# A padded 33rd head: zeros by GpSimd in place of 20 matmul columns per product

## The chip, the cores and the metric

The kernel runs on one core of a Trainium2 chip. The metric is the device time of one execution in microseconds; the median of three runs is given. A profiled execution shows what each engine did: TensorE (PE, with its weight loads as PEld), VectorE (DVE), ScalarE (ACT), GpSimd (POOL) and SyncE (SP, which issues the DMAs).

## The reference

One block of 2048 tokens with 640 features goes through a linear attention (A) and a gated feed-forward network (B), and a sigmoid gate for each token mixes the two. All inputs are bf16.

```python
qkv = (x @ wqkv).reshape(B, S, 3, H, Dh)                # H = 32 heads of Dh = 20
pq = einsum("bhsd,hdf->bhsf", q, w_phi)
pk = einsum("bhsd,hdf->bhsf", k, w_phi)
phi_q = concatenate([softmax(pq), softmax(-pq)], -1)    # 40 features a head
phi_k = concatenate([softmax(pk), softmax(-pk)], -1)
kv = einsum("bhsf,bhsd->bhfd", phi_k, v)
num = einsum("bhqf,bhfd->bhqd", phi_q, kv)
den = einsum("bhqf,bhf->bhq", phi_q, phi_k.sum(s)) + 1e-6
a = (num / den).reshape(B, S, D) @ wo
b = (silu(x @ w_gate) * (x @ w_up)) @ w_down            # F = 1728
g = sigmoid((x * gate_w).sum(-1))
out = g * a + (1 - g) * b
```

## The kernel before

**Tiles and stages.** Tokens are worked in 16 tiles of 128, in 4 blocks of 512. x lies transposed in `xT` (640 features as 5 chunks of 128 partitions). A short `premult` stage multiplies the k and q weights by `w_phi`, so that `wqk` turns x directly into the features' logits. For each block come 4 v tiles, 4 k tiles and the k-v product, summed in `kvacc`; from some 120 us on come 16 q tiles. The feed-forward network (`ffn`: gate and up for 14 column blocks, `down`) runs over the same 4 blocks in between, as the low-priority work of TensorE.

**A k or q tile** (`features`, L799). TensorE multiplies the token tile by `wqk[:, which]`: 5 matmuls of 512 columns into one PSUM bank and 5 short ones into the next. The bank pair is read as 33 heads of 20 logits (`HP = 33`, `pv` and `pg`, 660 columns), in 11 groups of 3 heads (`NG = 11`, `GH = 3`), since a group's 3 x 40 = 120 features fit 128 partitions once transposed. There are only 32 heads. For the 33rd place the first of the short matmuls is 148 columns wide: `over` (L795) runs 20 columns on into the next chunk's weights, so that the place holds finite numbers. VectorE takes maximum and minimum of each head (L831, L835), subtracts them into the slot `phi` (L839, L843), ScalarE takes the exponential, VectorE the sums (L854) and reciprocals (L858), and GpSimd normalizes in place (`f_nm`, L864). Later the rows of the 33rd place are multiplied away by the mask `kvm`, or meet no column.

**What follows.** For k: `kvpart` multiplies 4 tiles' `phi` with `v1` in two halves, groups 0 to 5 and 6 to 10. For q: SP transposes the slot by DMA into `eT`, TensorE multiplies by `kvsb` (`num`), VectorE divides (L946 to L955), SP transposes `ob` into `oT`, TensorE multiplies by `wo`, and the result is mixed and stored.

**Order.** Nothing is placed by hand: every piece of work is a task with a cost in us, dependencies, a priority and buffers to take and give back (`_Plan`, L229). The planner goes through time, and each engine that is free takes the first task of its list that can start. Feature products also have an earliest time (`hold`, L812), and transposes get some slack on top of their cost. The order found this way is written into the instruction streams; at run time an engine waits only for semaphores. The tracker (`_Tracker.run`, L160) derives these waits from the addresses read and written, within one engine too. All TensorE work is issued by one helper (`mms`, L420), so its line is L434 everywhere; memsets are issued at L454, ScalarE's at L444, DMAs at L462. `pair` is a pair of PSUM banks, `st` one of 3 sets of maxima, sums and so on, `phi` one of 11 slots, `us` one of 3 buffers for the up half of the feed-forward network. The `st` set is given back when the task `norm` ends.

Of the kernel before, what the change touches and what calls it, by code (L numbers as in the profile page):

```python
# [6 lines left out]
P = 128  # L7
S_TOK = 2048
D = 640
H = 32  # L10
DH = 20
# [6 lines left out]
NG = 11  # L18
GF = GH * 2 * DH
# [16 lines left out]
class _Tracker:  # L36
# [123 lines left out]
    def run(self, eng, fn, reads=(), writes=(), semname=None, inc=None):  # L160
        rkeys = [self._key_of(a) for a in reads]
        wkeys = [self._key_of(a) for a in writes]
        need = {}

        def req(ev):
            if ev is None:
                return
            s, v = ev
            if v > need.get(s, 0):
                need[s] = v  # L170

        for k in rkeys:
            for kk in self._conflicts(k):
                req(self.lastw[kk])
        for k in wkeys:
            for kk in self._conflicts(k):
                req(self.lastw[kk])
                for s, v in self.readers[kk].items():
                    req((s, v))
        self._emit_waits(eng, need)  # L180
        ins = fn()
        if semname is None:
            semname = {"pe": "pe", "act": "act", "dve": "dve", "pool": "pool"}[eng]
            if inc is None:
                inc = 1
        elif semname == "dma":
            semname = self.new_dma_sem()
            inc = 16
        ins.then_inc(self.sem[semname], inc)
        self.cnt[semname] += inc  # L190
        v = self.cnt[semname]
        ev = (semname, v)
        snapd = dict(self.known[eng])
        if snapd.get(semname, 0) < v:
            snapd[semname] = v
        self.evknow.setdefault(semname, {})[v] = snapd
        for k in wkeys:
            self.lastw[k] = ev
            self.readers[k] = {}
        for k in rkeys:  # L200
            r = self.readers[k]
            if r.get(semname, 0) < v:
                r[semname] = v
        return ev
# [24 lines left out]
class _Plan:  # L229
# [11 lines left out]
    def add(self, eng, cost, fn, deps=(), prio=5.0, lat=None, acq=(), rel=(), name=""):  # L241
        t = _Task(eng, cost, fn, deps, prio, self.LAT[eng] if lat is None else lat,
                  tuple(acq), tuple(rel), len(self.tasks), name)
        self.tasks.append(t)
        return t
# [82 lines left out]
def _mm(*cols):  # L328
    return sum(c / 2400.0 + 0.003 for c in cols)


def _build(
# [13 lines left out]
    pe, act, dve, pool, sp = nc.tensor, nc.scalar, nc.vector, nc.gpsimd, nc.sync  # L346
# [8 lines left out]
    def sb(name, shape, dtype):  # L355
        t = nc.alloc_sbuf_tensor(name, list(shape), dtype)
        tr.reg_tensor(t, "sbuf", nc.lookup_mloc(t).addr, rowelems(shape), mybir.dt.size(dtype))
        return t
# [6 lines left out]
    xT = sb("xT", [P, 5, S_TOK], BF16)  # L365
    wqk = sb("wqk", [P, 2, 5, D], BF16)
# [7 lines left out]
    phi = sb("phi", [P, NPHI, NG, P], BF16)  # L374
# [27 lines left out]
    ps = nc.alloc_psum_tensor("ps", [P, 8 * 512], F32)  # L402
# [6 lines left out]
    add = plan.add  # L409

    def bank(i, j, c0, c1, r0=0, r1=P):
        return ps[r0:r1, (2 * i + j) * 512 + c0:(2 * i + j) * 512 + c1]
# [4 lines left out]
    def wide(i, n=D):  # L417
        return ps[:, 2 * i * 512:2 * i * 512 + n]

    def mms(groups):  # L420

        reads = [g[1] for g in groups] + [g[2] for g in groups]
        writes = []
        seen = set()
        for g in groups:
            k = (g[0].offset, str(g[0].ap))
            if k not in seen:
                seen.add(k)
                writes.append(g[0])

        def fn():
            last = None
            for o, l, r, st, sp_ in groups:
                last = pe.matmul(o, lhsT=l, rhs=r, start=st, stop=sp_, skip_group_check=True)  # L434
            return last
        run("pe", fn, reads=reads, writes=writes)

    def acc(o, pairs):
        n = len(pairs)
        return [(o, l, r, i == 0, i == n - 1) for i, (l, r) in enumerate(pairs)]  # L440
# [8 lines left out]
    def poolop(fn, reads, writes):  # L449
        run("pool", fn, reads=reads, writes=writes)  # L450

    def memset(t_ap, val, eng):
        eobj = {"pool": pool, "dve": dve}[eng]
        run(eng, lambda: eobj.memset(t_ap, val), reads=[], writes=[t_ap])  # L454
# [81 lines left out]
    xl = [x_[4] for x_ in xs]  # L536
# [253 lines left out]
                        reads=[gtan[:, q]], writes=[gs[:, w, q]])  # L790
            gs_t[bt] = add("act", 0.2, gsf, deps=[g_], prio=2, name="gs")

    wflat = wqk[:, :, :, :].rearrange("p w c f -> p (w c f)")

    def over(which):  # L795
        c0 = which * 5 * D + 512
        return wflat[:, c0:c0 + P + DH]

    def features(t, which, wq_l, prio, ctx):  # L799

        tok = slice(t * P, (t + 1) * P)
        bt = t // 4

        def fn():
            mms(acc(bank(ctx["ps"], 0, 0, 512), [(xT[:, c, tok], wqk[:, which, c, 0:512]) for c in range(5)]) +
                [(bank(ctx["ps"], 1, 0, P + DH), xT[:, 0, tok], over(which), True, False)] +
                [(bank(ctx["ps"], 1, 0, P), xT[:, c, tok], wqk[:, which, c, 512:D], False, c == 4) for c in range(1, 5)])
        m_ = add("pe", _mm(*([512] * 5 + [148] + [128] * 4)), fn, deps=[xl[bt]] + wq_l, prio=prio,  # L810
                 acq=[("pair", ctx, "ps"), ("phi", ctx, "phi"), ("st", ctx, "st"), ("pp", ctx, "pp")], name="p" + str(which))
        m_.hold = K_AT + K_EACH * t if which else Q_AT + Q_EACH * t  # L812

        def dst():
            return phi[:, ctx["phi"], :, 0:GF]

        def pv():
            return wide(ctx["ps"], HP * DH).rearrange("p (h f) -> p h f", f=DH)

        def pg():  # L820
            return wide(ctx["ps"], HP * DH).rearrange("p (g k f) -> p g k f", k=GH, f=DH)

        def sv(sg):
            return dst().rearrange("p g (k s f) -> p g k s f", s=2, f=DH)[:, :, :, sg, :]

        def bc(tile):
            return tile[:, ctx["st"], :].rearrange("p (g k) -> p g k", k=GH).unsqueeze(3).to_broadcast([P, NG, GH, DH])

        def f_mx():
            a, b = mx[:, ctx["st"], :], pv()  # L830
            dveop(lambda: dve.tensor_reduce(a, b, AX.X, ALU.max), [b], [a])  # L831

        def f_mn():
            a, b = mn[:, ctx["st"], :], pv()
            dveop(lambda: dve.tensor_reduce(a, b, AX.X, ALU.min), [b], [a])  # L835

        def f_sp():
            o_, a, b = sv(0), pg(), bc(mx)
            dveop(lambda: dve.tensor_tensor(o_, a, b, ALU.subtract), [a, mx[:, ctx["st"], :]], [o_])  # L839

        def f_sn():
            o_, a, b = sv(1), bc(mn), pg()
            dveop(lambda: dve.tensor_tensor(o_, a, b, ALU.subtract), [b, mn[:, ctx["st"], :]], [o_])  # L843
        age = 2.5 + 0.01 * (t + (0 if which else NT))
        a1 = add("dve", 0.75, f_mx, deps=[m_], prio=age, name="max")
        a2 = add("dve", 0.75, f_mn, deps=[m_], prio=age, name="min")
        a3 = add("dve", 0.75, f_sp, deps=[a1, a2], prio=age, name="sub")
        a4 = add("dve", 0.75, f_sn, deps=[a2, a3], prio=age, rel=[("pair", ctx, "ps"), ("pp", ctx, "pp")], name="sub")
        x1 = add("act", 1.2, lambda: actop(dst(), dst(), ACTF.Exp), deps=[a4], prio=2, name="exp")

        def f_sm():
            a = sm[:, ctx["st"], :].rearrange("p (g k) -> p g k", k=2 * GH)
            b = dst().rearrange("p g (k f) -> p g k f", f=DH)
            dveop(lambda: dve.tensor_reduce(a, b, AX.X, ALU.add), [b], [a])  # L854

        def f_rc():
            a, b = rc[:, ctx["st"], :], sm[:, ctx["st"], :]
            dveop(lambda: dve.reciprocal(a, b), [b], [a])  # L858

        def f_nm():  # L860
            a = dst().rearrange("p g (k f) -> p g k f", f=DH)
            r = rc[:, ctx["st"], :]
            b = r.rearrange("p (g k) -> p g k", k=2 * GH).unsqueeze(3).to_broadcast([P, NG, 2 * GH, DH])
            poolop(lambda: pool.tensor_tensor(a, a, b, ALU.mult), [a, r], [a])  # L864
        b1 = add("dve", 1.45, f_sm, deps=[x1], prio=age, name="sum")
        b2 = add("dve", 0.47, f_rc, deps=[b1], prio=age, name="rec")
        return add("pool", 2.38, f_nm, deps=[b2], prio=1, rel=[("st", ctx, "st")], name="norm")

    kctx = {}

# [187 lines left out]
```

## Time and profile before

| What | Value |
|---|---|
| Median of 3 runs | 289.60 us (289.57 to 289.64) |
| The profiled execution | 289.35 us |
| its span, first to last instruction | 287.2 us |
| Granted TensorE clock | 1.0 |
| TensorE busy | 281.4 us, 98% of the span |
| VectorE busy | 224.6 us, 78% |
| GpSimd busy | 166.7 us, 58% |
| ScalarE busy | 144.5 us, 50% |
| GpSimd: normalizations | 32, 2426 ns each |
| GpSimd: products of gate and up | 56, 1154 ns each |

The page gives each engine's busy time, then 40 slices of the span in which a digit is the busy share in tenths, then the chain of work that ended last. Groups of instructions read: line, engine, operation, output<-inputs, shapes, count, then busy us, mean ns of one, and idle time of the engine before them. Timeline rows read: start in us from the span's start, length in us, engine, line, operation, output<-inputs, and how many instructions in a row were merged (the shape is that of the first). The end of a matmul is modelled, so its length is a latency; how fast TensorE goes is read from one start to the next. Some matmul records are missing from the trace; weight loads are complete.

### The profile page before, as it was taken

Reading aid. Unit: us, or ns where it says so; the run is one execution under the profiler, and the core shown is the slowest. Engines: PE = TensorE matmul, PEld = TensorE weight load, DVE = VectorE, ACT = ScalarE, POOL = GpSimd, SP = SyncE. Lnnn points to the kernel's source line nnn. Section 1 sums busy time; section 2 is a strip of 40 time slices with the busy share of each in tenths; the row PEclk is TensorE's granted clock in tenths of the full one; section 3 lists DMA queues with packets and bytes.
Section 4 is the critical chain, followed back from the end, with each engine's and each line's share of the span. In section 5 each row is a group of like instructions: output and inputs, shape, how many; then the busy total and the mean of one; then the engine's idle time right before and its main releaser. Section 6 shows DMA issues by size and latency. Waiting matters only on the chain.

```text
span 287.2 us, 5141 instructions
## 1 busy us (share of the span) xinstructions
PE 281.4 (98%) x2028; PEld 152.0 (53%) x2065; DVE 224.6 (78%) x317; ACT 144.5 (50%) x222; POOL 166.7 (58%) x131
## 2 busy tenths in 40 slices
PE   8999999999999999999999999999999999999996
PEld 2445554555555556555555655554555555555654
DVE  1323498999999998999997779999988897970212
ACT  2546376674865553445445354664664545564110
POOL 5397117677486457565667448688676566655100
PEclk9999999999999999999999999999999999999999
DMA  7999997000000000000234375134444433134211
GB/s 181 237 279 290 244 281 244 1 3 0 2 0 2 0 2 0 2 0 2 50 73 99 61 110 119 40 73 101 80 96 75 96 59 84 29 75 74 71 46 46
DMA packets 65415, 23.90 MB, mean 83 GB/s; under 512 B 53936, under 2 KB 65392, under 8 KB 65392
## 3 DMA queue, kind: packets, MB, share of 16 engines
q1 hardware_dynamic: 64736, 23.58, 36.3%
q8 instruction: 16, 0.26, 0.4%
q10 hardware_dynamic: 656, 0.00, 0.1%
q14 instruction: 7, 0.06, 0.1%
HBM read 8.30 MB, written 2.62 MB: 38 GB/s over the span
## 4 chain that ended last, share of the span: by engine, by line
PE 89%; DVE 9%; issue 1%
PE ps L434 89%; DVE sm L854 2%; DVE hT L611 1%; DVE phi L839 1%; DVE mx L831 1%; DVE mn L835 1%; DVE phi L843 1%; DVE rc L858 1%; DVE kvacc L904 0%; DVE xsb L690 0%; DVE us L454 0%
## 5 line engine op out<-in xcount | busy, mean ns | idle before, releaser
L864 POOL TENSOR_TENSOR phi<-phi,rc 128x1320 bf16<-128x1320 bf16 x32 | 77.6, 2426 | 32.5 <-DVE rc L858 32.5
L617 POOL TENSOR_TENSOR hT<-hT,us 128x512 bf16<-128x512 bf16 (+1 forms) x56 | 64.2, 1154 | 48.8 <-DVE hT L611 29.1
L434 PE MATMUL ps<-xT,wg 128*128 128x512 bf16 x268 | 67.6, 381 | 0.8
L434 PE MATMUL ps<-xT,wu 128*128 128x512 bf16 x256 | 64.2, 379 | 0.2
L434 PE MATMUL ps<-wd,hT 128*128 128x512 bf16 (+1 forms) x443 | 62.5, 298 | 0.3
L854 DVE TENSOR_REDUCE sm<-phi 128x66 f32<-128x1320 bf16 x32 | 48.6, 1518 | 9.5 <-ACT phi L444 9.3
L444 ACT ACTIVATE hT<-ps 128x512 bf16<-128x512 f32 (+1 forms) x56 | 33.2, 594 | 42.1 <-PE ps L434 41.9
L611 DVE SCALAR_TENSOR_TENSOR hT<-hT,ps 128x512 bf16<-128x512 bf16 (+1 forms) x56 | 37.8, 678 | 20.1 <-ACT hT L444 20.0
L444 ACT ACTIVATE phi<-phi 128x1320 bf16<-128x1320 bf16 x32 | 41.6, 1300 | 21.2 <-DVE phi L843 21.2
L434 PEld LDWEIGHTS ps<-wd,hT 128*128 128x128 bf16 x448 | 35.3, 98 | 28.3
L434 PE MATMUL ps<-wqk,xT 128*128 128x512 bf16 (+2 forms) x313 | 47.4, 298 | 0.4
L444 ACT ACTIVATE us<-ps 128x512 bf16<-128x512 f32 (+1 forms) x56 | 33.3, 596 | 17.5 <-PE ps L434 15.8
L434 PEld LDWEIGHTS ps<-xT,wu 128*128 128x128 bf16 x260 | 25.4, 98 | 30.7 <-issue 0.8
L434 PEld LDWEIGHTS ps<-xT,wg 128*128 128x128 bf16 x280 | 25.4, 98 | 24.6 <-issue 1.7
L434 PEld LDWEIGHTS ps<-wqk,xT 128*128 128x128 bf16 x320 | 26.5, 98 | 21.9
L831 DVE TENSOR_REDUCE mx<-ps 128x33 f32<-128x660 f32 x32 | 26.5, 828 | 5.1 <-PE ps L434 5.0
L704 POOL TENSOR_TENSOR xsb<-xsb,xb 128x640 bf16<-128x640 bf16 x12 | 16.8, 1396 | 19.4 <-ACT xb L444 19.4
L843 DVE TENSOR_TENSOR phi<-mn,ps 128x660 bf16<-128x660 f32 x32 | 26.5, 828 | 0.5
L835 DVE TENSOR_REDUCE mn<-ps 128x33 f32<-128x660 f32 x32 | 26.4, 825 | 0.0
L839 DVE TENSOR_TENSOR phi<-ps,mx 128x660 bf16<-128x660 f32 x32 | 26.2, 819 | 0.0
L444 ACT ACTIVATE xsb<-ps,gs 128x640 bf16<-128x640 f32 x16 | 12.6, 789 | 24.4 <-PE ps L434 24.4
L434 PE MATMUL ps<-wo,oT 128*128 128x512 bf16 (+1 forms) x154 | 23.0, 296 | 0.4
(44 smaller groups left out, 183.8 us busy)
## 6 DMA issues: line engine op xcount, KB each, us to landing
out_dram<-xsb SPq DMA_DIRECT2D x15, 160.0 KB, 1.8
wd<-in_B_w_down_dram SPq DMA_DIRECT2D x1, 2080.0 KB, 9.5
wg<-in_B_w_gate_dram SPq DMA_DIRECT2D x3, 320.0 KB, 3.7
wu<-in_B_w_up_dram SPq DMA_DIRECT2D x3, 320.0 KB, 4.3
wvg<-in_A_wqkv_dram SPq DMA_DIRECT2D x1, 800.0 KB, 7.7
wo<-in_A_wo_dram SPq DMA_DIRECT2D x1, 800.0 KB, 10.3
wg<-in_B_w_gate_dram SPq DMA_DIRECT2D x1, 640.0 KB, 4.7
wu<-in_B_w_up_dram SPq DMA_DIRECT2D x1, 640.0 KB, 6.0
```

Of the source, the lines that this page charges most:

```text
L434: last = pe.matmul(o, lhsT=l, rhs=r, start=st, stop=sp_, skip_group_check=True)
L444: run("act", lambda: act.activation(o, i, func, scale=scale), reads=reads, writes=[o])
L611: dveop(lambda: dve.scalar_tensor_tensor(out=hap, in0=hap, scalar=1.0, in1=g_, op0=ALU.add, op1=ALU.mult), [hap, g_], [hap])
L617: poolop(lambda: pool.tensor_tensor(hap, hap, u_, ALU.mult), [hap, u_], [hap])
L704: poolop(lambda: pool.tensor_tensor(x_, x_, b_, ALU.add), [x_, b_], [x_])
L831: dveop(lambda: dve.tensor_reduce(a, b, AX.X, ALU.max), [b], [a])
L835: dveop(lambda: dve.tensor_reduce(a, b, AX.X, ALU.min), [b], [a])
L839: dveop(lambda: dve.tensor_tensor(o_, a, b, ALU.subtract), [a, mx[:, ctx["st"], :]], [o_])
L843: dveop(lambda: dve.tensor_tensor(o_, a, b, ALU.subtract), [b, mn[:, ctx["st"], :]], [o_])
L854: dveop(lambda: dve.tensor_reduce(a, b, AX.X, ALU.add), [b], [a])
L858: dveop(lambda: dve.reciprocal(a, b), [b], [a])
L864: poolop(lambda: pool.tensor_tensor(a, a, b, ALU.mult), [a, r], [a])
```

## The change

The first short matmul of a k or q product now has 128 columns like the others, and the five form an ordinary accumulation. Nothing writes the 20 columns of the 33rd place any more; VectorE still reads them, with whatever an earlier user of the bank left there. Behind the normalization, in the same task, GpSimd writes zeros over the 40 features of that place in the `phi` slot. In the planner, a product costs 20 columns less and the task `norm` 2.52 us instead of 2.38.

```diff
-    wflat = wqk[:, :, :, :].rearrange("p w c f -> p (w c f)")
-
-    def over(which):
-        c0 = which * 5 * D + 512
-        return wflat[:, c0:c0 + P + DH]
-
     def features(t, which, wq_l, prio, ctx):
...
             mms(acc(bank(ctx["ps"], 0, 0, 512), [(xT[:, c, tok], wqk[:, which, c, 0:512]) for c in range(5)]) +
-                [(bank(ctx["ps"], 1, 0, P + DH), xT[:, 0, tok], over(which), True, False)] +
-                [(bank(ctx["ps"], 1, 0, P), xT[:, c, tok], wqk[:, which, c, 512:D], False, c == 4) for c in range(1, 5)])
-        m_ = add("pe", _mm(*([512] * 5 + [148] + [128] * 4)), fn, deps=[xl[bt]] + wq_l, prio=prio,
+                acc(bank(ctx["ps"], 1, 0, P), [(xT[:, c, tok], wqk[:, which, c, 512:D]) for c in range(5)]))
+        m_ = add("pe", _mm(*([512] * 5 + [128] * 5)), fn, deps=[xl[bt]] + wq_l, prio=prio,
...
             poolop(lambda: pool.tensor_tensor(a, a, b, ALU.mult), [a, r], [a])
+            memset(phi[:, ctx["phi"], NG - 1, GF - 2 * DH:GF], 0.0, "pool")
...
-        return add("pool", 2.38, f_nm, deps=[b2], prio=1, rel=[("st", ctx, "st")], name="norm")
+        return add("pool", 2.52, f_nm, deps=[b2], prio=1, rel=[("st", ctx, "st")], name="norm")
```

## The prediction

> **What bounds the kernel.** I read the profile's page first: the span, the busy time by engine, the 40 slices and the chain that ended last.
>
> ```profile
> span 287.2 us, 5141 instructions
> ...
> PE 281.4 (98%) x2028; PEld 152.0 (53%) x2065; DVE 224.6 (78%) x317; ACT 144.5 (50%) x222; POOL 166.7 (58%) x131
> ...
> PE   8999999999999999999999999999999999999996
> ...
> POOL 5397117677486457565667448688676566655100
> ...
> PE 89%; DVE 9%; issue 1%
> ```
>
> TensorE is busy in every slice but the first and the last, and the chain is TensorE for 89% of the span. "Busy" alone does not prove that it streams without a hole, since the end of a matmul is modelled. So I took the spacing of starts from the timeline of TensorE, in the stage where VectorE has most to do:
>
> ```profile
> 46.25 1.53 PE L434 MATMUL ps<-wqk,xT 128*128 128x512 bf16 x10
> 47.62 1.24 PE L434 MATMUL ps<-xT,wg 128*128 128x512 bf16 x5
> 48.70 1.24 PE L434 MATMUL ps<-xT,wu 128*128 128x512 bf16 x5
> ```
>
> Five matmuls of 512 columns start 48.70 - 47.62 = 1.08 us apart, 216 ns each. Going through all the starts of the trace, and allowing for missing records, I find after 6.5 us one hole over 12 ns beyond this spacing: 50 ns, at 41.4 us. So the end is set by how many columns TensorE streams, by the first 6.5 us (load landings) and by what follows the last matmul (284.9 to 287.2 us, the last addition and store). No q or k product runs before 31.7 us, so the head can't move; the last store is not touched.
>
> **What is removed.** 20 of the 148 columns of one matmul in each of 32 products (16 k, 16 q). The groups by shape:
>
> ```profile
> L434 PE MATMUL ps<-wqk,xT 128*128 128x128 bf16 x128 | 12.4, 219 | 0.0
> ...
> L434 PE MATMUL ps<-wqk,xT 128*128 128x148 bf16 x32 | 7.3, 228 | 0.1
> ```
>
> One takes 228 ns, the other 219: 9 ns, rounded. The starts agree: in the trace the next matmul begins 64 ns after a 128x148 and 56 ns after a 128x128, and the product above took 1.37 - 1.08 = 0.29 us for its five short ones (64 + 4 x 56 = 288 ns). So 8 ns x 32 = **0.26 us less**, on the path, as TensorE has no hole into which it could fall. The number of matmuls, weight loads and waits on TensorE stays.
>
> [...]
>
> **What is added.** One GpSimd memset of 128x40 bf16 behind each of the 32 normalizations, and a wait: the kernel's tracker makes it wait for the normalization's own semaphore, because it overwrites what that wrote. The trace has no memset of this size; its neighbours on GpSimd:
>
> ```profile
> L864 POOL TENSOR_TENSOR phi<-phi,rc 128x1320 bf16<-128x1320 bf16 x32 | 77.6, 2426 | 32.5 <-DVE rc L858 32.5
> ...
> L454 POOL MEMSET phi<- 128x968 bf16 x1 | 0.9, 905 | 0.3 <-POOLq L1042 0.3
> ...
> L454 POOL MEMSET kvm<- 128x126 bf16 x3 | 0.6, 210 | 0.0
> ...
> L1042 POOL MEMSET const-bfloat16-1.0<- 128x1 bf16 x1 | 0.1, 102 | 0.0
> ```
>
> Between 128x1 (102 ns) and 128x126 (210 ns) lie 108 / 125 = 0.86 ns an element, so 102 + 39 x 0.86 = about 135 ns, an estimate. Bounds: 0.10 us below, 0.91 us above (the 968-element row, however far). For the wait, a copy and two selects in place, each needing what the one before wrote:
>
> ```profile
> 12.77 0.30 POOL L551 COPY wbd<-wph 128x140 bf16<-128x140 bf16 x1
> 13.15 0.35 POOL L552 TENSOR_SCALAR_AFFINE_SELECT wbd<-wbd 128x140 bf16<-128x140 bf16 x1
> 13.57 0.35 POOL L555 TENSOR_SCALAR_AFFINE_SELECT wbd<-wbd 128x140 bf16<-128x140 bf16 x1
> 13.87 0.30 POOL L551 COPY wbd<-wph 128x140 bf16<-128x140 bf16 x1
> ```
>
> The dependent ones begin 0.07 us after the end of the one before (13.15 against 13.07), the independent copy 0.05 us before it (13.87 against 13.92). So the memset adds 0.07 + 0.135 = 0.205 us between the normalization's end and its own; bounds 0.17 and 0.98 us. GpSimd gets 32 x 0.2 = 6.6 us more (bounds 5.4 and 31): 166.7 becomes 173, at most 198, of 287. That is hidden as long as nobody waits for the 0.2 us. Who could:
>
> (a) On GpSimd the next instruction is queued behind it, mostly the product of gate and up (L617). It frees a us buffer, for which ScalarE's copy waits, which frees a PSUM bank for TensorE. The waits on that edge total 1.5 us in 2 cases, and no hole on TensorE came of them.
>
> (b) The k-v product. Its first half (groups 0 to 5) does not read the zeroed features and waits for the normalization alone, as now; its second half comes some 2 us later. The tightest of the four, in block 1:
>
> ```profile
> 81.81 2.43 POOL L864 TENSOR_TENSOR phi<-phi,rc 128x1320 bf16<-128x1320 bf16 x1
> ...
> 84.19 1.16 POOL L617 TENSOR_TENSOR hT<-hT,us 128x512 bf16<-128x512 bf16 x1
> 84.42 0.96 PEld L434 LDWEIGHTS ps<-v,phi 128*128 128x128 bf16 x24
> ```
>
> The weights load 84.42 - 84.24 = 0.18 us after the normalization, that is, just behind its semaphore, and the second half at 86.65 us has 2.4 us.
>
> (c) For a q tile, SP's transpose of phi into eT follows the memset, and num follows the transpose. Of 16 tiles the tightest is tile 8:
>
> ```profile
> 196.78 2.42 POOL L864 TENSOR_TENSOR phi<-phi,rc 128x1320 bf16<-128x1320 bf16 x1 [1.01 <-DVE rc L858]
> ...
> 199.23 1.40 SPq L462 DMA_TRANSPOSE eT<-phi  x1
> ```
> ```profile
> DMA to landing us min/median/max: 3.5/3.5/5.2
> ```
> ```profile
> 205.11 0.62 PEld L434 LDWEIGHTS ps<-kvsb,eT 128*128 128x128 bf16 x12
> ```
>
> This one is the 5.2 us transpose: 199.23 + 5.2 = 204.45 us, so 0.66 us are left, against 0.2 that are taken. Tile 4 has 1.0 us, all others 1.7 to 4.2. Behind SP's wait stand an oT transpose or an output store; wo has 1.4 us or more after each oT. At the upper bound (0.98 us) tile 8 alone would stall TensorE, by 0.3 us.
>
> VectorE keeps every instruction: it still reads 660 columns, the last 20 now being what an earlier user left in the bank. ScalarE and SP get no instruction more.
>
> **What is moved.** The planner books 2.52 instead of 2.38 us for a normalization and 0.008 us less for a product, so the order of all engines after the first k product may come out otherwise. The st buffer comes free 0.14 us later in the plan; in the trace the q product at 176.1 us loads weights 0.18 us after the normalization that gave up its buffer, so such a product may slip behind one gate and up pair, 2 x 1.08 = 2.16 us. That costs nothing by itself, since TensorE does the pair meanwhile; six `down` groups of 3.8 us remain as cover for the last q tile, whose num has 4.2 us left. I take 0 for the reordering: the present order, planned with the same latencies, has 320 reuses of a PSUM bank by TensorE, 24 of them under 0.3 us after the release by the trace, and they gave one hole of 50 ns. Bounds: 0.05 us gained (that hole), and as loss the rival below.
>
> **The sum.** Against the profiled execution, 289.35 us (span 287.2 and 2.15 around it): -0.26 + 0 + 0 = 289.09. The median of the runs stands 0.25 above that execution, so 289.60 - 0.26 = **289.34 us**, 0.09% less. What a measurement of this kernel can tell from no change is about 0.2%, 0.58 us: this is "same".
>
> **Rivals.**
> 1. *Slower: a num lands in the plan ahead of its transpose.* Place: the q stage, 143 to 268 us. If the new order moves a num up by one gate and up pair (2.16 us), a tile with the common 2.0 to 2.7 us stalls 0 to 0.3 us, and one like tile 8 stalls 2.16 - 0.66 + 0.2 = 1.7 us: 289.34 + 1.7 = 291.0. It decides from 0.58 + 0.26 = 0.84 us of stall on. With two or three smaller stalls the same mechanism gives about 290.3. For it: a transpose's landing varies from 3.5 to 5.2 us, and the plan can't know which. Against: the plan leaves room for that, and 15 of the 16 have 1 us or more now.
> 2. *No saving*: the weight load, not the columns, sets the pace of the short matmuls, and the time stays 289.6. Against: 64 and 56 ns between starts.
> 3. *Faster by over 0.2%.* The holes that could be closed come to 0.05 us, so the trimmed columns and the hole give 289.29. More must come from the 2.3 us after the last matmul, of which I can see no 0.3 that moves: 288.9 at best.
>
> **Chances.** The forecast 0.66, no saving 0.08, slower 0.22, faster 0.04. Faster by over 0.2%: 0.04; within: 0.66 + 0.08 = 0.74; slower: 0.22. The likeliest case alone reaches from 289.2 (the hole closed, and the 0.07 us by which runs differ) to 289.9 (the upper price of the memset at tile 8, and a bank or two late by 0.2 us). The range adds the smaller stalls of rival 1: 289.1 to 290.6.
>
> **What would show it.** The 128x148 group is gone and 160 matmuls of 128x128 stand at 219 ns; ten matmuls of a product take 1.36 us from start to start of the next; the memset has a row of 32 with 0.12 to 0.15 us, each about 0.07 us behind its normalization; TensorE's starts have no new hole, and its last matmul ends near 284.6 us. I am wrong if a num or k-v weight load waits visibly for a DMA or GpSimd, if bank waits add up to 0.8 us, or if VectorE's rows grow beside the memsets.

## The result and the profile after

The changed kernel takes 288.75 us (median of 8 runs, 288.46 to 289.03) against 289.61 for the kernel before on the same chip: ratio 0.9973, 95% interval 0.9964 to 0.9982. That is 0.86 us less, where 0.26 was forecast; the time lies under the forecast's range. Its profiled execution took 288.79 us with a span of 287.07, against 289.35 and 287.19 before. So in these two executions the span fell by 0.12 us, and what lies around it by 0.44, from 2.16 to 1.72 us.

The page of the kernel after:

```profile
span 287.1 us, 5211 instructions
...
PE 283.3 (99%) x2065; PEld 151.7 (53%) x2065; DVE 224.8 (78%) x317; ACT 144.7 (50%) x222; POOL 170.7 (59%) x163
...
PE 99%; DVE 0%; issue 0%
```

TensorE still binds. (Its busy time reads higher because this trace lacks no matmul record: 2065 instead of 2028. Its share of the last chain, 99% where it was 89%, is no gain in time either: the span fell by 0.12 us.) The groups by shape show the two edits at the sizes forecast:

```profile
L434 PE MATMUL ps<-wqk,xT 128*128 128x128 bf16 x160 | 14.2, 219 | 0.0
...
L454 POOL MEMSET phi<- 128x40 bf16 x32 | 4.2, 131 | 1.9
```

160 short matmuls stand at 219 ns and the 148-column group is gone. The memset takes 131 ns and waits 1.9 / 32 = 0.06 us behind its normalization, 0.19 us together, where 0.205 was estimated. The timeline of TensorE around the same k product:

```profile
46.36 1.52 PE L434 MATMUL ps<-wqk,xT 128*128 128x512 bf16 x10
47.72 1.24 PE L434 MATMUL ps<-xT,wg 128*128 128x512 bf16 x5
48.80 1.24 PE L434 MATMUL ps<-xT,wu 128*128 128x512 bf16 x5
```

The product takes 1.36 us from start to start instead of 1.37. The last matmul ended at 284.74 us and not near 284.6, because the first k product began 0.18 us later than before, at 31.88 us. From the first k weight load to the end of the last matmul, which I call the body, it was 284.74 - 31.88 = 252.87 us (starts unrounded), against 284.86 - 31.70 = 253.16 before: 0.29 us less, 0.26 of it columns. The rest of the gain is not in the body. What lies behind the last instruction is seen by asking for the DMA queues from the end of the span on. The kernel before, 287.2 to 290 us, first the share of the DMA engines in 40 slices of 0.07 us:

```profile
DMA  0000000000000030000000000000000000000000
...
DMA packets 1, 0.01 MB, mean 3 GB/s; under 512 B 0, under 2 KB 0, under 8 KB 0
...
q14 instruction: 1, 0.01, 1.0%
```

The same view of the kernel after, from its own end on:

```profile
DMA packets 0, 0.00 MB, mean 0 GB/s; under 512 B 0, under 2 KB 0, under 8 KB 0
```

One packet of the instruction queue, 8192 bytes, starts in the 15th slice, at 288.19 us, 1.0 us after the last profiled instruction, and took 0.44 us. The kernel after has no such packet there; it has one more inside the program (8 of this queue where the kernel before has 7). From the name of the queue I took it that its packets are blocks of an engine's code, which no view shows. This made theory 1: the 32 memsets shift the places at which GpSimd's instructions are fetched in blocks, and the last fetch no longer falls behind the end. The rivals: theory 2, the new order brings the rest; theory 3, the 20 columns are worth more than 8 ns; theory 4, the two kernels differ by chance in the first 7 us.

### The profile page after: what moved, and what is told of

The parts are those of the page before. It is cut to its first block, busy times and chain, and to the rows that moved or that the text cites. A ratio compares the mean times of both kernels' runs of the same rounds, so it can differ in the third digit from the quotient of the medians.

```text
span 287.1 us, 5211 instructions
## 1 busy us (share of the span) xinstructions
PE 283.3 (99%) x2065; PEld 151.7 (53%) x2065; DVE 224.8 (78%) x317; ACT 144.7 (50%) x222; POOL 170.7 (59%) x163
## 4 chain that ended last, share of the span: by engine, by line
PE 99%; DVE 0%; issue 0%
PE ps L434 99%; DVE xsb L690 0%; DVE us L454 0%
## 5 line engine op out<-in xcount | busy, mean ns | idle before, releaser
L434 PE MATMUL ps<-xT,wg 128*128 128x512 bf16 x280 | 70.2, 381 | 0.1
L434 PE MATMUL ps<-wqk,xT 128*128 128x512 bf16 (+1 forms) x320 | 48.5, 299 | 0.0
L434 PE MATMUL ps<-wo,oT 128*128 128x512 bf16 (+1 forms) x160 | 24.2, 299 | 0.0
```

## The experiments

Every run lists its time and its span, so each kernel has a mean span and a mean of what lies outside it (time minus span; both in us below). The body comes from each profile.

| Kernel | Ratio (95% interval) | Span, mean; before on that chip | Outside, mean | Body in the profile | Packet behind the end |
|---|---|---|---|---|---|
| before, unchanged | 1.0000 (0.9991 to 1.0009) | 287.35; 287.35 | 2.15 | 253.17 | yes |
| 8 small memsets more | 0.9991 (0.9983 to 1.0000) | 287.52; 287.35 | 1.73 | 253.25 | no |
| narrow alone | 0.9993 (0.9984 to 1.0002) | 287.12; 287.35 | 2.17 | 252.90 | yes |
| zeros alone | 0.9996 (0.9987 to 1.0005) | 287.55; 287.35 | 1.71 | 253.19 | no |
| changed kernel | 0.9971 (0.9960 to 0.9983) | 287.13; 287.53 | 1.71 | 252.87 | no |
| new order alone | 0.9996 (0.9988 to 1.0005) | 287.42; 287.53 | 2.15 | 253.12 | yes |
| change, old order | 0.9979 (0.9970 to 0.9988) | 287.27; 287.53 | 1.75 | 252.93 | no |
| change and 96 memsets | 1.0000 (0.9985 to 1.0015) | 287.56; 287.53 | 2.15 | 252.87 | yes |
| narrow, 8 memsets, no zeros | 0.9973 (0.9963 to 0.9984) | 287.16; 287.45 | 1.73 | 252.85 | no |
| 8 instructions fewer | 0.9986 (0.9978 to 0.9995) | 287.48; 287.45 | 1.73 | 253.17 | no |
| changed kernel again | 0.9974 (0.9964 to 0.9983) | 287.12; 287.45 | 1.73 | 252.86 | no |

The standard error of a mean span is 0.04 to 0.08 us (0.21 for the kernel with 96 memsets: two of its 11 runs took 1.6 us longer in the span, and the cause is open). Outside the span no single run is further than 0.08 us from its kernel's mean. Differences below are taken before rounding.

**The kernel before, unchanged**

> The kernel before, unchanged, to see the spans of its runs and what lies outside the span. Theory 1 (the change shortens what lies outside the span, because GpSimd's last block of instructions is no longer fetched behind the program's end): span near 287.4, 2.15 us outside it in every run, and an 8192-byte packet of the instruction queue about 1 us behind the last instruction. Theory 2 (the new order), 3 (a column costs more than 8 ns per 20) and 4 (noise of the head) expect about 1.7 us outside and so spans near 287.9. All expect a ratio of 1.000.

11 runs gave a mean of 2.15 us outside, as did 33 runs of the same kernel beside them. So the missing 0.43 us is a steady property of the two programs, and theories 2 to 4, which are about the span, can't hold it.

**Eight small memsets more**

```diff
-    pad_t = add("pool", 0.7, lambda: memset(phi[:, :, :, GF:P], 0.0, "pool"), prio=2.9, name="pad")
+    def pad_fn():
+        memset(phi[:, :, :, GF:P], 0.0, "pool")
+        for _ in range(8):
+            memset(phi[:, 0, 0, GF:GF + 2], 0.0, "pool")
+    pad_t = add("pool", 0.7, pad_fn, prio=2.9, name="pad")
```

> The kernel before with 8 more tiny memsets on GpSimd in the first 12 us, where it idles; nothing else differs, no column is removed. Theory 1: the packet of the instruction queue moves from behind the end into the program, outside the span 1.7 instead of 2.15 us, so -0.45 us, ratio 0.9985. Theories 2, 3 and 4: 0, ratio 1.000.

Outside the span 1.73 us, as theory 1 says, with not one column removed. The view of this kernel's DMA queues from its end on:

```profile
DMA packets 0, 0.00 MB, mean 0 GB/s; under 512 B 0, under 2 KB 0, under 8 KB 0
```

The packet is now inside, at 258.1 us, as the view from 257 to 259 us shows:

```profile
DMA  0000000000000000000000500000000000000000
...
q14 instruction: 1, 0.01, 1.4%
```

The trace also points to an engine. Of the 8 packets of 8192 bytes that this queue moved in the kernel before while it ran and just behind, only two moved with the eight memsets, from 61.6 to 51.9 us and from 288.2 to 258.1; the other six stayed within 0.4 us. Between the two that moved the trace has 128 records of GpSimd in the kernel before and 127 here, waits for semaphores included. Behind the second it has none in the kernel before, 8 here and 31 in the changed kernel, which has 32 more. So the two packets lie 128 GpSimd records apart, as far as these counts can show it, and theory 1 reads this as a block of 128.

Its span was 0.16 us longer, so the total came out at -0.26 us by the means and not -0.43. In the profile the body is under 0.1 us longer, and TensorE has one hole of that size, where wo waited for a transpose of ob that took 4.7 us to land instead of the usual 2.6:

```profile
256.26 0.52 PE L434 MATMUL ps<-kvsb,eT 128*128 128x63 bf16 x12
...
256.69 1.36 PEld L434 LDWEIGHTS ps<-wo,oT 128*128 128x128 bf16 x10
...
256.92 1.30 PE L434 MATMUL ps<-wo,oT 128*128 128x512 bf16 x9
```

There are ten weight loads and nine matmuls: the record of the first is missing, so it began 0.22 us ahead of the 256.92 shown, 0.08 us later than the stream would have had it. Whether that is the same in each run the profile of one can't tell.

**The narrow matmul alone**

```diff
...
-                [(bank(ctx["ps"], 1, 0, P + DH), xT[:, 0, tok], over(which), True, False)] +
-                [(bank(ctx["ps"], 1, 0, P), xT[:, c, tok], wqk[:, which, c, 512:D], False, c == 4) for c in range(1, 5)])
+                acc(bank(ctx["ps"], 1, 0, P), [(xT[:, c, tok], wqk[:, which, c, 512:D]) for c in range(5)]))
```

> The change's narrow matmul alone: 128 columns instead of 148, no zeros behind the normalization (the 33rd place keeps what came of an earlier user of the bank), the planner's costs and so the order as before. Theory 1: -0.26 us in the span, still 2.15 us outside it, ratio 0.9991. Theory 2: -0.26. Theory 3: the whole -0.86, ratio 0.997.

Span -0.24 us with an error of 0.07, body -0.26, outside 2.17. The columns are worth what their spacing says (in the kernel before, the next start 64 ns behind a 128x148 and 56 behind a 128x128), and theory 3, which expected -0.86, falls.

**The zeros alone**

```diff
             poolop(lambda: pool.tensor_tensor(a, a, b, ALU.mult), [a, r], [a])
+            memset(phi[:, ctx["phi"], NG - 1, GF - 2 * DH:GF], 0.0, "pool")
```

> The change's memset alone: zeros behind each normalization, matmuls 148 columns wide and the planner's costs as before. GpSimd has 32 instructions more. Theory 1: span unchanged, outside it 1.7 us, -0.45 us, ratio 0.9985. Theories 2 and 3: 0 or, if somebody waits for the 0.2 us of each memset, slower.

Outside 1.71 us, body 253.19 against 253.17: the 32 memsets and their waits cost TensorE nothing. The span was 0.20 us longer on average all the same, with an error of 0.09, so the total came out at -0.24 us by the means where theory 1 expected -0.45; in the profile that lies ahead of the first k product (32.17 against 31.79 us). The profiles of all kernels here put that product between 31.70 and 32.21 us, so this may be chance; it isn't settled.

**The changed kernel, for comparison**

> The changed kernel itself, beside the three below on one chip. Columns and fetch alone (each run by itself so far: -0.23 us of span, -0.43 us outside it): -0.66 us, span 287.1 where the kernel before has 287.35, ratio 0.9977. If the new order gains too (theory 2): span 286.9 or less, ratio 0.997 or less.

-0.80 us by the medians, with -0.40 in the span and -0.46 outside it.

**The new order alone**

```diff
-        m_ = add("pe", _mm(*([512] * 5 + [148] + [128] * 4)), fn, deps=[xl[bt]] + wq_l, prio=prio,
+        m_ = add("pe", _mm(*([512] * 5 + [128] * 5)), fn, deps=[xl[bt]] + wq_l, prio=prio,
...
-        return add("pool", 2.38, f_nm, deps=[b2], prio=1, rel=[("st", ctx, "st")], name="norm")
+        return add("pool", 2.52, f_nm, deps=[b2], prio=1, rel=[("st", ctx, "st")], name="norm")
```

> The new order alone: the planner is told the change's costs, the matmuls keep 148 columns and there are no zeros. Theory 2 (the new order): about -0.2 to -0.3 us in the span, 2.15 us outside it, ratio 0.999. Columns and fetch alone: 0, or a little slower where the planner's costs no longer fit.

Body -0.05 us, which is the size of the hole at 41.4 us, gone here; span -0.11 with an error of 0.06. Theory 2 keeps about a tenth of a microsecond, of which 0.05 is seen in the trace.

**The change in the old order**

Here and in the next experiment the edit is against the changed kernel.

```diff
-        m_ = add("pe", _mm(*([512] * 5 + [128] * 5)), fn, deps=[xl[bt]] + wq_l, prio=prio,
+        m_ = add("pe", _mm(*([512] * 5 + [148] + [128] * 4)), fn, deps=[xl[bt]] + wq_l, prio=prio,
...
-        return add("pool", 2.52, f_nm, deps=[b2], prio=1, rel=[("st", ctx, "st")], name="norm")
+        return add("pool", 2.38, f_nm, deps=[b2], prio=1, rel=[("st", ctx, "st")], name="norm")
```

> The change with the planner's old costs: 128 columns, zeros, and the order of before. Columns and fetch alone: as the changed kernel, -0.66 us, 1.72 us outside the span. Theory 2: 0.2 to 0.3 us more than the changed kernel, all of it in the span.

-0.26 us in the span, 1.75 outside: columns and fetch, nothing else. The body is 0.06 us above that of the new order.

**The change and 96 small memsets**

```diff
...
+        for i in range(96):
+            memset(phi[:, i // NG, i % NG, GF:GF + 2], 0.0, "pool")
```

> The changed kernel with 96 more tiny memsets on GpSimd in the first 12 us, where it idles, so that its instructions end at the same place of a block of 128 as in the kernel before (32 + 96 = 128). Theory 1 (fetch behind the end): the packet is back about 1 us behind the last instruction, 2.15 us outside the span, +0.43 us against the changed kernel. If the number of GpSimd's instructions has nothing to do with it: 1.72 us outside, as the changed kernel.

This is the sharpest of the tests: the same zeros, the same columns, the same body, but 32 + 96 = 128 instructions more on GpSimd than in the kernel before. The view from the end of its span, 287.4 us, on:

```profile
DMA  0000000000000050000000000000000000000000
...
DMA packets 1, 0.01 MB, mean 3 GB/s; under 512 B 0, under 2 KB 0, under 8 KB 0
...
q14 instruction: 1, 0.01, 1.3%
```

The packet is back behind the end, 2.15 us lie outside the span, and the median of 289.46 us is 0.57 above the changed kernel's: 0.44 lie outside the span, the rest in it.

**Narrow, eight memsets, no zeros**

This takes the narrow matmul and the eight memsets from above, and tells the planner of the narrow product alone.

> A try at beating both kernels: 128 columns, no zeros behind the normalization (the 33rd place keeps what came of an earlier user of the bank), and 8 tiny memsets on GpSimd in the first 12 us instead; the planner is told the narrower product and the old cost of a normalization, so its order is a third one. Columns and fetch alone: -0.26 in the span, -0.43 outside it, 0 or 0.05 from the order: as the changed kernel within 0.1 us, so no gain over it. If the zeros cost something on the path: faster than the changed kernel by that.

288.88 us beside 288.80: no gain over the change. The body is 252.85 us against 252.86, so the zeros cost nothing on TensorE's path that shows here, though the order differs too. No version here beats the changed kernel.

**Eight instructions fewer**

```diff
-        poolop(lambda: pool.tensor_copy(d_, s_), [wph[:, c, :]], [d_])
+        dveop(lambda: dve.tensor_copy(d_, s_), [wph[:, c, :]], [d_])
...
-        memset(d_, 1.0, "pool")
+        memset(d_, 1.0, "dve")
```

> The kernel before with 8 of GpSimd's instructions of the first 18 us given to VectorE (three memsets of the mask, five copies of w_phi). GpSimd's stream then ends 8 places earlier in its block. Theory 1: the fetch moves behind the program altogether or falls away, if what GpSimd runs behind the last profiled instruction is shorter than 8: 1.7 us outside, -0.43 us; if it is longer, the packet stays behind the end and 2.15 us with it. The span is as before within 0.1 us.

1.73 us outside and no packet behind the end, with fewer instructions instead of more. GpSimd has 11 records fewer in the trace, the 8 operations and 3 semaphore instructions. The packet that came at 61.6 us now comes at 82.1, and 116 records follow it instead of 128, so by theory 1 the stream ends before the next block is asked for. VectorE has 8 operations more here, so this kernel alone could not tell the two engines apart; the memsets above touched GpSimd alone. It gained 0.31 us by the medians (ratio 0.9986, 0.9978 to 0.9995) with all computation unchanged.

**The changed kernel again**

> The changed kernel again, on the chip of the two beside it and for more runs: span 0.31 us under the kernel before (0.26 columns, 0.05 order), 1.72 us outside it; ratio 0.9974.

-0.33 us in the span, 1.73 outside.

## Why the prediction was wrong

**The step that failed** is in the sum: "Against the profiled execution, 289.35 us (span 287.2 and 2.15 around it)". The 2.15 us were carried over as a constant, which puts the change of what lies outside the span at nothing without a reason. It measured -0.43 us: 2.15 with a packet of the instruction queue behind the end, 1.72 without. In these runs that packet went and came with the number of GpSimd's instructions (gone with 8 or 32 more and with 8 operations fewer, back with 128 more), and the change adds 32. The prediction counted these as GpSimd's time (6.6 us, hidden) and not as instructions. Rival 3, faster by over 0.2%, is what came about, with a chance of 0.04: it looked only at the 2.3 us between the last matmul and the end of the span and allowed "288.9 at best". The trace had the row, the instruction packet at 288.19 us, outside the span that the slices cover.

**What was right.** The mechanism on TensorE and its size: 0.26 us forecast, body -0.26 for the narrow matmul alone. Rival 2, no saving, falls with the same run. The memset: 0.19 us with its wait against 0.205, and hidden: in the changed kernel a num still waits for no transpose. Tile 8, the tightest before, reads in the timeline of the kernel after:

```profile
199.01 2.42 POOL L857 TENSOR_TENSOR phi<-phi,rc 128x1320 bf16<-128x1320 bf16 x1
201.49 0.13 POOL L454 MEMSET phi<- 128x40 bf16 x1
```
```profile
201.65 1.40 SPq L462 DMA_TRANSPOSE eT<-phi  x1
```
```profile
207.20 0.62 PEld L434 LDWEIGHTS ps<-kvsb,eT 128*128 128x128 bf16 x12
```

The transpose is issued 0.22 us after the normalization's end, where it was 0.03 before, by the memset and its wait, and landed at 205.18 us, 2.0 us before its num. The tightest is now tile 12 with 0.8 us. The tile itself moved: 2.2 us later, as the reordering could do. The order cost nothing and closed the hole of 50 ns, its lower bound; from the first k product on, the largest hole is now 32 ns, ahead of a k-v product at 133.5 us. Rival 1 did not come about.

**The sum as measured**: columns -0.26, order -0.05, outside the span -0.43, together -0.74 us. The three comparisons of the changed kernel gave -0.86, -0.80 and -0.75 by their medians. The remaining 0.0 to 0.1 us lies within the scatter of the first 32 us, in which the profiles of one and the same kernel differ by 0.1 us and those of all kernels by 0.5.

## What to carry to other kernels

On TensorE, which here had no hole over 50 ns behind its first 6.5 us, the spacing of starts priced the trimmed columns (0.26 us forecast, 0.26 measured in the body), and 0.19 us more on GpSimd behind each normalization cost nothing where each consumer had more than that left (0.66 us at the tightest in the kernel before; body 253.19 us with the zeros alone, 253.17 without). But the time measured is more than the span: compare both, run by run, and look at the DMA packets behind the last instruction. Here an instruction packet stood there, and 8 instructions more or fewer on GpSimd were worth more than the trimmed columns: of 2.15 us outside the span 1.73 were left, against 0.26 us of columns. In the total times of the three kernels that have this alone (8 memsets more, zeros alone, 8 instructions fewer) 0.2 to 0.3 us of it was left by the medians, since two of them had longer spans, which is not settled. The engine the packet goes with was found by adding instructions to one engine alone: 8 on GpSimd moved it from 288.2 to 258.1 us.

## What the runs showed of the hardware

The packet behind the end went and came with GpSimd's count: 32 or 8 instructions more, or 11 records fewer, removed it, 128 more brought it back, with 2.10 to 2.23 us outside the span where it is there and 1.67 to 1.80 where it is not, in every run. A period of 128 fits these counts and the 128 records between the two packets that moved; that GpSimd's code is fetched in blocks of that size is theory 1's reading of them, and no view shows what a packet holds. In all profiles the packets of the queue that carries it have 8192 bytes from the first microsecond on, those of the other instruction queue 16384. Inside the program TensorE showed nothing of such a packet: in the changed kernel the one that goes with GpSimd lies at 225.9 us and took 0.56 us, and TensorE had no hole there over the 32 ns at 133.5 us. What behind the profiled end asks for the packet, and why the program's end is later by 0.43 us where it is there, is open: in the five profiles that have the packet it took 0.44 to 0.56 us, and the time outside the span did not follow its length.
